# Weight conversion at the start of a fused attention and feed-forward kernel: a third buffer for raw words, exponents through PSUM, rows on two queues, one piece begun ahead

## The chip, the core and the metric

The kernel runs on one core of a Trainium2 chip. The metric is the device time of the whole program in microseconds (us), the median of several runs. The profile is one execution on that core, taken by the hardware profiler. The engines are TensorE (PE in the profile; PEld is its weight load), VectorE (DVE), ScalarE (ACT), GpSimd (POOL) and SyncE (SP, which here only issues transfers).

## The reference

Inputs q, k, v are 8 x 8 x 576 x 64 in float32: batch, heads, sequence, head size. For each batch and head:

```python
scores = scale * np.matmul(q, k.transpose(0, 1, 3, 2))
kth = np.partition(scores, -32, axis=-1)[..., -32:-31]
scores = np.where(scores >= kth, scores, -1000000000.0)
attn = softmax(scores)           # max subtracted, 1e-09 in the divisor
out = np.matmul(attn, v)
```

The heads are put side by side, which gives x of 4608 x 512, and then comes a feed-forward block with weights w_in (512 x 2048) and w_out (2048 x 512):

```python
h = x @ w_in
g = h - np.tanh(h)
y = g @ w_out
```

Each row of scores keeps only what is at least its 32nd largest value. The two weights are handed over as float64. [...] the kernel takes the two 32-bit words of each float64 apart and puts a float32 together.

## The kernel before, in words

**Steps.** The work is cut into 144 steps. A step is a pair of heads and a tile of 128 query rows (or, for the 64 rows that are left over, two pairs of heads). All orders are written out by hand: `run` goes over n from -4 to NS + 3, and in each round emits one stage of several steps: the scores of step n + 1 (`scores`, L224, matmul L233, copy out of PSUM L241), the search of step n (`search`, L244), the mask of step n - 1 (`mask`, L280: tb L290, z L303 on ScalarE and L306 on GpSimd, bad L310), its exponentials (`expo`, L322, L326), the transpose of step n - 2 (on TensorE in `turn_pe`, L389: matmuls L404 and copies L407; or on VectorE in `turn_z`, L365, and `spread_keys`, L377), and the product with v (`values`, L414, matmuls L428, the reciprocals' transpose L436, copy L440, xT L452). [...]

**The search** is VectorE's main work. It takes the minimum and maximum of the two halves of the scores (L263, L264), then four rounds of max (L271) and match-replace (L274), each of which gives the eight next largest. After each of the four rounds it calls `between(i)`, which emits what was planned for that gap: transposes of k and q rows (`turn_rows`, L218), and parts of the weight conversion.

**Feed-forward work** is a list (`work`) of small items (`ffn_h`, matmuls L481, tanh L493, copy L494, subtraction L495; `ffn_o`, matmuls L502, copy L512). `deal` gives them out between the stages, at the rate that `rate` computes from what is due. An item isn't given out before the weight pieces that it uses are converted: `converted[0]` counts these.

**The weight conversion** (`convert`, L136). A piece is 128 rows by 512 columns; there are 32: 0 to 15 are w_in, 16 to 31 w_out. A piece needs a place for raw words (a "slot") with two halves, one for the words as they are and one for the same bytes shifted by three. SyncE issues the two loads (L146, L147). Part 1 of the piece, emitted later: VectorE takes sign and exponent bits out of the high words (L156, into f), ScalarE turns them into a float32 exponent with two instructions (L157 and L158, both from f into f), VectorE takes the mantissa bits from the shifted words (L160), ScalarE scales these (L163). Part 2: VectorE joins sign and exponent (L166, with the raw words and f as inputs, f as output), and GpSimd multiplies both (L169). Part 2 frees the slot, and `load_piece` (L600) at once takes the first free slot that the next piece may use and emits its loads.

**Slots** (L128 to L134). Two slots lie in the tile `spare`, which serves as a transposition buffer later; four lie in the parts of w_out that aren't converted yet. Each has a bound: a slot in w_out[j] may be used only by pieces before that part is itself filled, that is before piece 16, 20, 24 or 28; a slot in `spare` by any piece. `load_piece` takes the first usable slot in the list. So pieces 28 to 31 have only the two slots of `spare`. `zx2` (L115) holds two transposition buffers for later: the first in its own tile, the second in `spare`.

**The plan of the conversion** is `many`: two pieces in step 0, two in step 1, three in each of the steps 2 to 9, four in step 10. Within a step, the parts are spread over the four gaps of the search.

**The start.** Before the first search come, on SyncE's queue: four loads each of the first k rows and q rows (`load_rows`, L196; a row load is 72 KB in runs of 128 bytes), the loads of piece 0, the next k and q rows, piece 1, and so on. The PSUM pool `h_ps` has two buffers with the tag "h", which only the feed-forward products use.

Of the kernel before, what the change touches and what calls it, by code (L numbers as in the profile page):

```python
# [8 lines left out]
AF = mybir.ActivationFunctionType  # L9
ALU = mybir.AluOpType  # L10
FP32 = mybir.dt.float32
I32 = mybir.dt.int32
U32 = mybir.dt.uint32
# [35 lines left out]
def kernel(  # L49
# [9 lines left out]
    nc = tc.nc  # L59
    P = nc.NUM_PARTITIONS  # L60
# [7 lines left out]
    CD = DM // P  # L68
# [6 lines left out]
    WJ = 4  # L75
    FJ = CF // WJ
    scale = 1.0 / float(D) ** 0.5
# [5 lines left out]
    def pool(name, bufs, **kw):  # L83
        return ctx.enter_context(tc.tile_pool(name=name, bufs=bufs, **kw))
# [15 lines left out]
    h_ps = pool("h_ps", 2, space=PS)  # L100
# [9 lines left out]

    NW = 512


    spare = consts.tile([P, 4, NW, 2], U32, name="spare")
    later = spare[:].rearrange("p a n w -> p (a n w)").bitcast(FP32)  # L115
    zx2 = [consts.tile([P, 4 * S], FP32, name="zx")[:], later[:, 0 : 4 * S]]
# [3 lines left out]
    e255 = consts.tile([P, 1], FP32, name="e255")  # L120
    nc.gpsimd.memset(e255[:], 255.0 * 2.0**23)

    def flat(x):
        return x.rearrange("p n w -> p (n w)")

    slots = [(spare[:, i], spare[:, 2 + i], 8 * CD) for i in range(2)]  # L128
    for j in reversed(range(WJ)):
        halves = [  # L130
            flat(w_out[j][:, 2 * i : 2 * i + 2, :]).bitcast(U32).rearrange("p (n w) -> p n w", w=2)
            for i in range(2)
        ]
        slots.append((*halves, (WJ + j) * CD))  # L134

    def convert(piece, slot):  # L136


        j, i = piece // CD, piece % CD
        if j < WJ:  # L140
            src, dst = moe_w_in[i * P : (i + 1) * P, j * NW : (j + 1) * NW], w_in[j][:, i, :]
        else:
            r0 = ((j - WJ) * FJ + i) * P
            src, dst = moe_w_out[r0 : r0 + P, :], w_out[j - WJ][:, i, :]
        raw, shifted, _ = slot
        nc.sync.dma_start(flat(raw), src.bitcast(U32))  # L146
        nc.sync.dma_start(  # L147
            flat(shifted).bitcast(U8)[:, 0 : 8 * NW - 4], src.bitcast(U8)[:, 3 : 8 * NW - 1]
        )
        yield  # L150
        hi = raw[:, :, 1]
        f = thpool.tile([P, NW], FP32, tag="th", name="f")
        fu = f[:].bitcast(U32)


        nc.vector.tensor_scalar(fu, hi, 20, 0x7FF, ALU.logical_shift_right, ALU.bitwise_and)  # L156
        nc.scalar.activation(f[:], fu, AF.Relu, bias=e1151[:], scale=-(2.0**23))  # L157
        nc.scalar.activation(f[:].bitcast(I32), f[:], AF.Relu, bias=e255[:], scale=-1.0)  # L158

        nc.vector.tensor_scalar(  # L160
            dst.bitcast(U32), shifted[:, :, 0], 0x0FFFFFFF, None, ALU.bitwise_and
        )
        nc.scalar.activation(dst, dst.bitcast(U32), AF.Copy, bias=1.0, scale=2.0**-28)  # L163
        yield

        nc.vector.scalar_tensor_tensor(  # L166
            out=fu, in0=hi, scalar=0x80000000, in1=fu, op0=ALU.bitwise_and, op1=ALU.bitwise_or
        )
        nc.gpsimd.tensor_tensor(dst, dst, f[:], ALU.mult)  # L169
        yield  # L170
# [15 lines left out]
    def load_rows(name, b, hp, exact):  # L186

        if b == 0 and hp and not exact:
            x = early[2 * hp - 2 + (name == "q")]
        else:  # L190
            x = ldpool.tile([P, S], FP32, tag=f"{name}in", name=f"{name}in")[:]
        raw[name, b, hp] = x
        src = {"k": k, "q": q}[name]
        for a in range(NG):
            h, d = 2 * hp + a // 2, a % 2 * G
            nc.sync.dma_start(  # L196
                x[a * G : (a + 1) * G, :].rearrange("i (n d) -> i n d", d=G),
                src[b, h, :, d : d + G].rearrange("(n i) d -> i n d", i=G),
            )
# [145 lines left out]
    def spread(n):  # L345

        if steps[n].last:
            rd = rds.pop(n)
            nq = steps[n].nq
            rx = rxs[n] = xpool.tile([P, 2, 2, D], FP32, tag="rx", name="rx")  # L350
            nc.gpsimd.tensor_copy(
                rx[:, 0:nq], rd[:, 0:nq].unsqueeze(3).to_broadcast([P, nq, 2, D])
            )
# [174 lines left out]
    steps, done, work = [], {}, []  # L528
# [38 lines left out]
    def run(exact):  # L567
# [4 lines left out]
        def at(n, fn):  # L572
            todo.setdefault(n, []).append(fn)
# [3 lines left out]
        for i, (b, hp) in enumerate(pairs):  # L577
            n = next(n for n, g in enumerate(steps) if (g.b, g.hp) == (b, hp))
# [18 lines left out]
        pieces = 0 if exact else 2 * WJ * CD  # L597
        free, loaded, converted = list(slots), [], [2 * WJ * CD - pieces]

        def load_piece():  # L600
            k = len(loaded)
            usable = [x for x in free if x[2] > k]
            if k < pieces and usable:
                free.remove(usable[0])
                piece = convert(k, usable[0])
                next(piece)
                loaded.append((piece, usable[0]))

        def part(x, k):
            next(loaded[k][0])  # L610
            if x == 2:
                converted[0] = k + 1
                free.append(loaded[k][1])
                load_piece()

        for _ in slots[NHP:]:
            at(-4, load_piece)
        started = 0
        for m in range(max(many) + 1 if pieces else 0):
            mine = range(started, min(started + many[m], pieces))  # L620
            started = mine.stop
            seq = [(1, k) for k in mine[:1]]
            for k in mine[1:]:
                seq += [(1, k), (2, k - 1)]
            seq += [(2, k) for k in mine[-1:]]
            for i, x in enumerate(seq):
                at_round.setdefault((m, 3 * i // max(len(seq) - 1, 1)), []).append(
                    lambda x=x: part(*x)
                )

        def here(i):
            return 0 <= n + i < NS

        def between(i):
            for fn in at_round.pop((n, i), []):
                fn()
            if i == 0 and here(-2):
                invert(n - 2)
                if not steps[n - 2].pe:
                    turn_z(n - 2)  # L640
# [9 lines left out]
        for u in begun:  # L650
            k = 2 if u.tag == "xT" else 1
# [5 lines left out]
        def rate():  # L657


            have, low, high = len(work), 0.0, None  # L660
            coming = sorted((t, u.n // 8) for u, t in ready.items() if t > n)
            for t, k in coming + [(NS + 4, 0)]:
                r = have / max(t - n, 1)
                high = r if high is None else min(high, r)
                have += k
            for u, t in begun.items():
                if t > n and u in before:
                    need = [i + 1 for i, x in enumerate(work) if x[1] is before[u]]
                    if need:
                        low = max(low, need[-1] / (t - n))  # L670
            return max(low, high)

        credit = 0.0

        def deal(part):
            nonlocal credit
            credit += part * share
            while work and credit > 0 and work[0][0] <= converted[0]:
                work.pop(0)[2]()
                credit -= 1  # L680
            credit = min(credit, 1.0)

        for n in range(-4, NS + 4):
            pe = here(-2) and steps[n - 2].pe
            if here(-3) and not steps[n - 3].pe:
                spread(n - 3)
            for m in (n - 4, n - 3):
                if 0 <= m < NS and steps[m].last and steps[m].lag == n - m:
                    values(m)
            share = rate()  # L690
            if pe:
                w = turn_pe(n - 2)
                next(w)
            if here(-1):
                mask(n - 1, exact)
            if here(0):
                search(n, exact, between)
            elif here(-2):
                between(0)
            if here(-2) and not pe and steps[n - 2].last:  # L700
                spread_keys(n - 2)
            if pe:
                spread(n - 2)
            deal(0.4)
            if here(1):
                scores(n + 1)
            if pe:
                next(w)
            if here(-1):
                expo(n - 1)  # L710
            deal(0.2)
            if pe and steps[n - 2].last:
                values(n - 2)
            deal(0.2)
            for fn in todo.pop(n, []):
                fn()
            deal(0.2)
# [4 lines left out]
    with tc.manual_schedule():  # L722
        run(False)
# [42 lines left out]
```

## Time and profile before

| | value |
|---|---|
| time, median of 3 runs | 1573.74 us (1572.37 to 1576.3) |
| span of the profiled execution | 1571.8 us |
| TensorE busy | 1463.9 us (93%) |
| VectorE busy | 1322.7 us (84%) |
| ScalarE busy | 907.7 us (58%) |
| GpSimd busy | 945.5 us (60%) |
| chain that ended last | TensorE 81%, VectorE 8%, ScalarE 4%, SyncE's queue 3%, GpSimd 2% |
| loads of w_in and w_out pieces, issue to landing | 4.2 to 6.2 us |

How to read it: busy time is an average over stages with different limits. The page cuts the span into 40 equal slices (39.3 us each) and gives the busy tenths of each engine: TensorE is at 2 to 7 tenths in the first five slices and at 8 or 9 from the sixth on. A row of a timeline gives start, duration, engine, line of the program, operation, out<-in and, in brackets, how long the engine had stood idle before it and which instruction or transfer ended that. Releasers are inferred from semaphore events; where an instruction waits for several, the one that came last by the profile is named.

### The profile page before, as it was taken

The numbers are of one execution on the slowest core, as the hardware profiler recorded it, in microseconds if no ns is written. First come the engines' busy times: TensorE is split into PE (matmuls) and PEld (weight loads), VectorE is DVE, ScalarE is ACT, GpSimd is POOL, SyncE is SP. The second block draws the span as 40 slices with busy tenths as digits, with TensorE's granted clock in tenths as the row PEclk, the third lists the DMA queues.
The fourth block names the chain that finished last, engine by engine and source line by source line (L and its number), as shares of the span: only waits on it lengthen the run. The fifth ranks groups of instructions, "written<-read, shape, count | busy, mean of one in ns | idle before, by whom it ended". The sixth has DMA issues, their size and how long they took to land.

```text
span 1571.8 us, 25605 instructions
## 1 busy us (share of the span) xinstructions
PE 1463.9 (93%) x7834; PEld 940.6 (60%) x7834; DVE 1322.7 (84%) x3810; ACT 907.7 (58%) x1637; POOL 945.5 (60%) x1533
## 2 busy tenths in 40 slices
PE   2566699899999999999999999999999999999998
PEld 1355376556566565656666565656666666666675
DVE  7987689999999999998999999998999899874300
ACT  4877577556556565656556565656555565654431
POOL 2777467657567575657467575756566565644521
PEclk9877799999999999999999999999999999999999
DMA  9844112333532334233432343333432334210000
GB/s 248 297 172 168 69 30 56 88 86 65 115 88 61 90 82 91 69 80 75 100 88 62 84 94 83 74 79 76 97 92 61 82 84 96 55 45 7 8 8 16
DMA packets 245009, 134.43 MB, mean 86 GB/s; under 512 B 205440, under 2 KB 205440, under 8 KB 244864
## 3 DMA queue, kind: packets, MB, share of 16 engines
q1 hardware_dynamic: 244864, 132.71, 34.7%
q8 instruction: 64, 1.05, 0.3%
q14 instruction: 81, 0.66, 0.1%
HBM read 61.85 MB, written 9.44 MB: 45 GB/s over the span
## 4 chain that ended last, share of the span: by engine, by line
PE 81%; DVE 8%; ACT 4%; SPq 3%; POOL 2%; DMA 1%; issue 1%; DVEq 0%; ACTq 0%; POOLq 0%
PE hps L481 29%; PE ops L502 29%; PE av L428 9%; PE scps L233 9%; PE zt L404 2%; DVE m L271 2%; DVE ab L274 2%; PE av L436 2%; SPq L196 1%; SPq L385 1%; DVE f L166 1%; ACT z L303 1%; DMA spare<-in_moe_w_out_dram 1%; ACT sc L241 1%; ACT f L157 1%
## 5 line engine op out<-in xcount | busy, mean ns | idle before, releaser
L502 PE MATMUL ops<-w_out,g 128*128 128x512 f32 x1152 | 524.7, 599 | 0.0
L481 PE MATMUL hps<-xT,w_in 128*128 128x256 f32 (+1 forms) x2304 | 476.0, 362 | 0.2 <-POOL xT L452 0.2
L271 DVE MAX8 m<-ab 128x8 f32<-128x288 f32 (+1 forms) x1152 | 464.9, 445 | 0.0
L306 POOL TENSOR_TENSOR z<-sc,z 128x576 f32<-128x576 f32 x288 | 400.0, 1411 | 106.3 <-ACT z L303 106.3
L481 PEld LDWEIGHTS hps<-xT,w_in 128*128 128x128 f32 x2304 | 399.2, 195 | 63.5 <-issue 14.4
L274 DVE MATCH_REPLACE8 ab<-m,ab 128x288 f32<-128x288 f32 x864 | 376.2, 443 | 0.0
L502 PEld LDWEIGHTS ops<-w_out,g 128*128 128x128 f32 x1152 | 210.9, 192 | 232.0 <-issue 229.7
L303 ACT ACTIVATE z<-sc,tb 128x576 f32<-128x576 f32 x288 | 207.8, 770 | 138.3 <-POOL tb L290 138.3
L495 POOL TENSOR_TENSOR g<-g,th 128x512 f32<-128x512 f32 x144 | 183.8, 1276 | 130.2 <-ACT g L494 126.3
L241 ACT COPY sc<-scps 128x1152 f32<-128x1152 f32 x144 | 160.9, 1117 | 121.5 <-PE scps L233 117.0
L326 ACT ACTIVATE z<-z,nb 128x576 f32<-128x576 f32 x288 | 221.7, 775 | 5.3 <-POOL z L306 5.2
L263 DVE TENSOR_TENSOR ab<-scps,sc 128x576 f32<-128x576 f32 x144 | 107.0, 743 | 133.2 <-POOL bad L310 73.3
L233 PE MATMUL scps<-kT,qT 64*128 64x288 f32 (+1 forms) x1280 | 185.5, 439 | 31.0 <-DVE qT L218 28.8
L233 PEld LDWEIGHTS scps<-kT,qT 64*128 64x128 f32 (+1 forms) x1280 | 100.5, 181 | 122.3 <-issue 65.5
L428 PE MATMUL av<-et,vb 128*64 128x256 f32 (+1 forms) x1152 | 133.5, 368 | 39.9 <-ACT et L407 34.2
L493 ACT ACTIVATE th<-hps 128x512 f32<-128x512 f32 x144 | 85.3, 592 | 114.7 <-PE hps L481 107.1
L452 POOL TENSOR_TENSOR xT<-xs 128x256 f32<-128x256 f32 (+1 forms) x72 | 48.0, 667 | 157.2 <-ACT xs L440 157.0
L428 PEld LDWEIGHTS av<-et,vb 128*64 128x64 f32 x1152 | 77.6, 140 | 100.2 <-ACT et L407 37.8
L440 ACT COPY xs<-av 128x512 f32<-128x512 f32 (+1 forms) x88 | 44.7, 508 | 154.9 <-PE av L436 154.8
L336 POOL TENSOR_SCALAR rd<-den 128x2 f32<-128x2 f32 x144 | 33.4, 232 | 146.7 <-ACT z L326 113.1
L266 DVE MAX8 ab<-ab 128x8 f32<-128x288 f32 x288 | 116.4, 445 | 0.0
L264 DVE TENSOR_TENSOR ab<-scps,sc 128x576 f32<-128x576 f32 x144 | 107.4, 746 | 0.0
(59 smaller groups left out, 1319.0 us busy)
## 6 DMA issues: line engine op xcount, KB each, us to landing
et<-spare SPq DMA_DIRECT2D x416, 72.0 KB, 2.0
et<-zx SPq DMA_DIRECT2D x416, 72.0 KB, 2.0
kin<-in_k_dram SPq DMA_DIRECT2D x116, 72.0 KB, 2.4
qin<-in_q_dram SPq DMA_DIRECT2D x116, 72.0 KB, 2.5
vb<-in_v_dram SPq DMA_DIRECT2D x64, 128.0 KB, 2.5
out_dram<-ot SPq DMA_DIRECT2D x32, 256.0 KB, 2.2
spare<-in_moe_w_out_dram SPq DMA_DIRECT2D x11, 512.0 KB, 4.2
spare<-in_moe_w_out_dram SPq DMA_DIRECT2D x11, 511.5 KB, 5.1
```

Of the source, the lines that this page charges most:

```text
L233: nc.tensor.matmul(ps[rows, t, s, 0:S2], qT[g.b, g.hp + i][half(t), qs], kT[g.b, g.hp + i][half(t), ks], start=True, stop=True,)
L241: nc.scalar.copy(sc[:], ps[:, :, :, 0:S2])
L266: nc.vector.max(ab[:, t, S2 : S2 + 8], lo[:, t, :])
L271: nc.vector.max(m[:, t, m8], last[t] if i == rounds - 1 else cur[t])
L274: nc.vector.match_replace(nxt[t], m[:, t, m8], cur[t], NEG)
L303: nc.scalar.activation(zv[:, t, :], scf[:, t, :], AF.Relu, bias=tb[:, t : t + 1], scale=-BIG)
L306: nc.gpsimd.tensor_tensor(zv[:, t, :], scf[:, t, :], zv[:, t, :], ALU.subtract)
L326: nc.scalar.activation(x["zv"][:, t, :], x["zv"][:, t, :], AF.Exp, bias=x["nb"][:, t : t + 1], scale=scale, accum_out=den[:, t : t + 1],)
L428: nc.tensor.matmul(av[half(t), 0, cols], vb[g.b, hp][:, t, c, :] if c < J else vr[g.b, hp][:, t, :], es[:, :, (J + 1) * t + c if c < J els ...
L481: nc.tensor.matmul(cur[u][:, s : s + w], w_in[j][:, c, fo : fo + P], u.xT[:, c, 0:w], start=(c == 0), stop=(c == CD - 1),)
L495: nc.gpsimd.tensor_tensor(g, g, th[:], ALU.subtract)
L502: nc.tensor.matmul(cur[u][:], u.g[o // 1024][:, o % 1024 // 512, o % 512 : o % 512 + P], w_out[f // FJ][:, f % FJ, :], start=(f == 0), sto ...
```

## The change

It has five parts, all in the conversion of weights and in the start. A third slot, `first`, lies in the first transposition buffer (`zx2[0]`), which isn't used before the conversion is over, so seven pieces instead of six can be under way, and three instead of two at the end; `load_piece` takes the usable slot with the earliest bound instead of the first of the list. For the pieces of w_in, L158 writes its exponents into a PSUM tile (`e`, from the pool `h_ps`) instead of into f, and L166 reads them there. Three of the four loads of the first q rows are issued by ScalarE instead of SyncE. Part 1 of piece 0 is emitted in round -1, before the first search, instead of in its first gap. And `deal` compares with the number of pieces converted before the round's search (`usable`) instead of with the number at that moment.

```diff
+    first = zx2[0][:, 0 : 4 * NW].bitcast(U32).rearrange("p (a n w) -> p a n w", a=2, w=2)
     slots = [(spare[:, i], spare[:, 2 + i], 8 * CD) for i in range(2)]
+    slots.append((first[:, 0], first[:, 1], 8 * CD))
...
         nc.scalar.activation(f[:], fu, AF.Relu, bias=e1151[:], scale=-(2.0**23))
-        nc.scalar.activation(f[:].bitcast(I32), f[:], AF.Relu, bias=e255[:], scale=-1.0)
+
+        e = h_ps.tile([P, NW], FP32, tag="h", name="e")[:] if j < WJ else f[:]
+        nc.scalar.activation(e.bitcast(I32), f[:], AF.Relu, bias=e255[:], scale=-1.0)
...
         nc.vector.scalar_tensor_tensor(
-            out=fu, in0=hi, scalar=0x80000000, in1=fu, op0=ALU.bitwise_and, op1=ALU.bitwise_or
+            out=fu, in0=hi, scalar=0x80000000, in1=e.bitcast(U32), op0=ALU.bitwise_and, op1=ALU.bitwise_or
         )
...
-            nc.sync.dma_start(
+            queue = nc.scalar if a and (name, b, hp, exact) == ("q", 0, 0, False) else nc.sync
+            queue.dma_start(
...
             if k < pieces and usable:
-                free.remove(usable[0])
-                piece = convert(k, usable[0])
+                slot = min(usable, key=lambda x: x[2])
+                free.remove(slot)
+                piece = convert(k, slot)
                 next(piece)
-                loaded.append((piece, usable[0]))
+                loaded.append((piece, slot))
...
+        if pieces:
+            at(-1, lambda: part(1, 0))
...
+            seq = [x for x in seq if x != (1, 0)]
...
-            while work and credit > 0 and work[0][0] <= converted[0]:
+            while work and credit > 0 and work[0][0] <= usable:
...
-            share = rate()
+            share, usable = rate(), converted[0]
```

## The prediction

> **What bounds the kernel now.** I read the busy shares in slices first, then busy time by stage, then the waits of VectorE in the first 200 us, then the timeline of single steps. First busy time in four stages; the columns are the stretch, its length, and busy us (instructions) of TensorE, its weight loads, VectorE, ScalarE and GpSimd, then TensorE's granted clock, DMA share and GB/s:
> ```profile
> 0.00:180.00 180.00, 91.08 (x493) 66.08 (x493) 143.30 (x376) 119.02 (x207) 106.44 (x143) 0.81 0.65 207
> 180.00:400.00 220.00, 208.34 (x1191) 135.34 (x1192) 212.74 (x632) 143.74 (x267) 149.01 (x252) 0.99 0.29 63
> 400.00:1400.00 1000.00, 999.68 (x5208) 623.63 (x5207) 927.38 (x2675) 582.81 (x1043) 629.06 (x1048) 1.00 0.37 82
> ```
> From 400 us TensorE has no gap and the change removes no matmul, so nothing is to be won there. From 180 to 400 us VectorE and TensorE are both near full, and that work is not touched either. What can be won is start-up, where TensorE idles 89 of 180 us while the weights are converted: if stage one ends X us sooner, all that follows starts X us sooner. So I count X.
>
> Start-up goes in steps, one search each; a step begins with L263. The same table by step, for steps 0, 1, 4 and 8 to 10 (step 0 begins at 11.76 us):
> ```profile
> 11.76:23.77 12.01, 2.29 (x8) 1.26 (x8) 12.01 (x32) 4.93 (x7) 1.26 (x1) 1.00 1.14 236
> 23.77:36.81 13.04, 3.52 (x14) 2.46 (x15) 12.44 (x33) 7.98 (x14) 7.04 (x9) 1.00 1.08 308
> ...
> 64.33:77.71 13.38, 7.23 (x41) 4.99 (x39) 12.75 (x35) 11.14 (x22) 10.79 (x13) 0.63 0.63 226
> ...
> 120.34:136.65 16.31, 12.13 (x86) 10.76 (x86) 12.84 (x34) 12.01 (x24) 12.15 (x15) 0.81 0.42 144
> 136.65:153.78 17.13, 11.22 (x63) 8.75 (x64) 12.76 (x34) 12.82 (x25) 12.06 (x15) 0.70 0.46 170
> 153.78:180.84 27.06, 12.32 (x38) 5.76 (x35) 14.52 (x38) 12.90 (x24) 10.96 (x14) 0.69 0.33 117
> ```
> VectorE fills steps 0 to 5 (12.75 of 13.38 us), idles 3 to 4 us in steps 7 to 9, and idles 12.5 us of 27.06 in step 10. Its waits up to 200 us say on what (us in total, times, longest):
> ```profile
> DVE f L166 <- ACT f L158: 17.3, 8, 4.4
> DVE f L156 <- DMA spare<-in_moe_w_out_dram: 6.0, 3, 3.3
> DVE kT L218 <- DMA kin<-in_k_dram: 4.9, 1, 4.9
> DVE ab L263 <- ACT sc L241: 3.9, 3, 3.5
> DVE w_out L160 <- DMA spare<-in_moe_w_out_dram: 2.3, 3, 0.8
> ```
> The second and fifth rows are step 10, waiting for raw words; the third and fourth are mostly the start of step 0. The first is 0.63 us a step up to step 6, then 2.8 to 4.4 us in steps 7 to 10. Last, VectorE's own rows around the end of step 3 (start, us):
> ```profile
> 61.79 0.67 DVE L166 SCALAR_TENSOR_TENSOR f<-w_out,f 128x512 uint32<-128x512 uint32 x1
> 62.38 0.82 DVE L271 MAX8 m<-ab 128x8 f32<-128x296 f32 x2
> 63.13 1.28 DVE L166 SCALAR_TENSOR_TENSOR f<-w_out,f 128x512 uint32<-128x512 uint32 x1
> 64.33 0.74 DVE L263 TENSOR_TENSOR ab<-scps,sc 128x576 f32<-128x576 f32 x1
> ```
> The same L166 takes 0.67 or 1.28 us. GpSimd's L169 ran from 62.59 to 63.86, and the slow L166 ends 0.55 us after it: it stood still until GpSimd was done. L263 has one operand in PSUM, runs beside the next L169 (64.54 on), and takes 0.74.
>
> [...] No row here has ScalarE writing PSUM; L158 into SBUF takes 0.72 us. [...] four row issues take 2.01 us on SyncE, and the DMA engines are already 0.78 to 0.91 busy from 2 to 5 us.
>
> **The change, part by part.** "Piece k" is the k-th of 32 weight pieces: 0 and 1 in step 0, 2 and 3 in step 1, then three a step, 28 to 31 in step 10.
>
> *Exponents by way of PSUM (pieces 0 to 15, steps 0 to 5).* L166 then has one SBUF input. Its price from the nearest row: L263, 576 elements in 0.74 us[...]. Nine of the 16 are slow now (1.30, 1.30, 1.30, 1.35, 1.28, 1.35, 1.29, 1.35, 1.27: 11.8 us), so 11.8 - 9 x 0.68 = 5.7 us of VectorE time goes. Is it on the path? In steps 3 to 5 two loops start at the end of a step's last L166: VectorE's own, 6.7 us to the next step's first L166 (64.33 to 71.0), and L169 (GpSimd), rx, the transposes (TensorE), et, z, L157, L158 (ScalarE), 7.2 us (64.41 to 71.64), the 0.63 us wait. Both begin earlier with it, and the two slow L166 lie between the loop's end and its next start, so both savings count whole: 3.8 us over steps 3 to 5. ScalarE then needs 11.1 of about 12.1 us, and the next L263 may wait 0.4 us for the scores' copy, inside the 0.5 us by which VectorE's loop is shorter. Step 2 has one slow L166: 0.6. Steps 0 and 1 are below. Bounds: 5.7 if all counts; about 1 if ScalarE's copy holds the step. L158 into PSUM: I take 0.72[...]. The exponents share two PSUM buffers with the first feed-forward product; a third L158 of a step must await the first L166, which precedes L156 of that piece on VectorE anyway: nothing. The first product comes after piece 15's step.
>
> *First q rows on two queues.* Three of four issues leave SyncE's queue: the last q row is issued 1.6 us sooner (3 x 0.53). But the DMA engines have only 0.22 + 0.20 + 0.09 + 0.11 + 0.05 + 0.08 = 0.75 us idle between 2 and 8 us. Bounds 0.3 and 1.6; I take 0.75. ScalarE's three issues (about 1.5 us) lie before its first copy at 10.61: nothing.
>
> *One piece begun ahead.* L156 and L160 of piece 0 (0.41 each) move into VectorE's 3.54 us gap before the first L263: 0.7 us off step 0. They wait for piece 0's words, behind which the first search stands on VectorE. DMA moves these words between 6 and 10.5 us now; with the 0.75 they land by 10, the scores by 11: no stall, by a small margin.
>
> But steps 0 and 1 can't keep it all: DMA is saturated (share 1.14, 1.08), and piece 3 is already awaited,
> ```profile
> DVE w_in L160 <- DMA w_out<-in_moe_w_in_dram: 0.6, 1, 0.6
> ```
> and its words still come behind the same transfers. So up to there only the 0.75 us is gained, the pair moved and piece 1's L166 going into this wait, and after it piece 3's L166 (0.6): 1.4 together.
>
> *A third place for raw words, tightest deadline first.* Following load_piece by hand: before, pieces 28 to 31 have two places, so 30 is issued after 28 is finished and 31 after 29. After, 30 is issued at the end of step 9, and only 31 in step 10, when 28 is finished. The issues and VectorE's waits now:
> ```profile
> 165.59 0.33 SPq L146 DMA_DIRECT2D spare<-in_moe_w_out_dram  x1
> 170.44 0.43 DVE L156 TENSOR_SCALAR f<-spare 128x512 uint32<-128x512 uint32 x1 [3.30 <-DMA spare<-in_moe_w_out_dram]
> 172.68 0.33 SPq L146 DMA_DIRECT2D spare<-in_moe_w_out_dram  x1
> 176.78 0.43 DVE L156 TENSOR_SCALAR f<-spare 128x512 uint32<-128x512 uint32 x1 [2.55 <-DMA spare<-in_moe_w_out_dram]
> ```
> Step 10 on today's clock: piece 28's L166 still ends at 165.55 (ScalarE's chain sets it, 4.28 us, not touched; the 0.91 us waits before it vanish into that). Then max and replace to 167.1, L156 and L160 of piece 30 to 167.8, L166 of 29 to 168.4, max and replace to 170.0; L156 of 31 waits to 170.44 and L160 to 171.63, as 30's did; L166 of 30 to 172.6, maxes to 173.3, L166 of 31 behind L169 to 174.6. Now 180.84: 6.2 us. Bounds: 3.3 + 0.8 = 4.1 if only the first wait goes, 7.35 if all four. In steps 6 to 9 every piece has 13 us or more to arrive, before and after. The new order sends seven pieces ahead, so the first v rows wait one more megabyte (2.7 us at the 377 GB/s of 36 to 40 us); they are awaited at 44.6 and issued by 34.2: hidden.
>
> *The limit taken before the search* (usable): the order of TensorE's and GpSimd's instructions that the changed kernel writes out is the old one, so nothing.
>
> Sum: 1.4 + 0.6 + 3.8 + 6.2 = 12.0; 1573.7 - 12.0 = 1561.7, said as 1562.
>
> **Rivals.** (a) Only step 10 gains, 6.2 + 0.5: 1567. For it: ScalarE is the next full engine, and DMA is saturated up to 60 us. Against: the loop starts at L166. (b) All gains at their upper bounds, 1.6 + 0.7 + 5.7 + 7.35 = 15.4: 1558.3. Against: piece 3's wait. (c) No change, 1572 to 1574: TensorE's low granted clock (0.63 to 0.9 before 180 us) shifts[...], and it gives back what was won. For: steps 7 to 9 do wait behind 3.6 us bursts of L481. Against: no such work is added. (d) Slower: L166 from PSUM always takes 1.35 (16 x 0.67 - 5.7 = +5), piece 0 stalls the first search by 2, and piece 31 lands so late that step 10 gives 3: 1578. Against: L263's 0.74.
>
> **How the numbers follow.** Forecast 0.55, (a) 0.20, (b) 0.15, (c) 0.07, (d) 0.03. Range 1556.5 to 1568: it holds the forecast and most of (a) and (b); the bounds of 4.1 to 7.35 and 1 to 5.7 reach no further. Faster by over 0.3% (4.7 us): forecast, (b), nearly all of (a), a little of (c): 0.90; within: 0.08; slower: 0.02.
>
> **What would show it.** Right: L166 at 0.68 for pieces 0 to 15 beside GpSimd, still 1.28 for later ones; steps 3 to 5 near 12.1 us; step 10 near 20.8 with one wait for raw words; steps 6 to 9 as before; TensorE gapless from about 390. Wrong: L263 waiting on L241 by more than 0.5 us in each step; L156 of piece 0 or 1 waiting over 1 us; steps 7 to 9 over 17.5 us.

## The result, and the profile after

The changed kernel takes 1561.93 us (median of 4 runs, 1561.04 to 1565.41). Runs of the kernel before, taken with it, have a median of 1573.05 us (1572.32 to 1576.3). The ratio is 0.9929, with a 95% interval of 0.9909 to 0.995: 11.2 us less, where 12 was forecast. The profiled execution has a span of 1560.3 us, against 1571.8.

First busy time by stage in the changed kernel, with stage borders 10 us earlier (columns as in the prediction):

```profile
0.00:170.00 170.00, 89.37 (x498) 65.34 (x499) 140.72 (x379) 121.21 (x212) 105.11 (x145) 0.82 0.67 219
...
390.00:1390.00 1000.00, 999.68 (x5218) 624.96 (x5215) 925.54 (x2669) 584.04 (x1042) 630.20 (x1050) 1.00 0.37 82
```

The first stage is 10 us shorter, and the busy time of the engines differs by 3 us at most. In the middle one, left out here, TensorE and VectorE are busy for 209.55 and 212.12 of 220 us (208.34 and 212.74 before), and the last is what it was. So what went from start-up is mostly idle time, and on VectorE some time in which a slow join (1.27 to 1.35 us instead of 0.67) counted as busy while it stood still. The steps of the changed kernel, 0, 1, 4 and 8 to 10:

```profile
10.82:21.80 10.98, 2.29 (x8) 1.27 (x8) 10.79 (x31) 4.91 (x7) 1.26 (x1) 1.00 1.09 244
21.80:34.77 12.97, 3.07 (x12) 2.01 (x13) 11.91 (x34) 7.90 (x13) 6.88 (x9) 1.00 1.06 302
...
60.96:73.12 12.16, 6.99 (x38) 4.75 (x38) 11.74 (x35) 11.14 (x22) 9.21 (x14) 0.64 0.78 290
...
115.06:131.69 16.63, 12.56 (x86) 11.20 (x86) 12.84 (x34) 12.11 (x24) 12.15 (x15) 0.80 0.35 126
131.69:148.04 16.35, 9.78 (x63) 7.30 (x64) 12.75 (x34) 12.81 (x25) 12.07 (x15) 0.82 0.47 176
148.04:168.40 20.36, 12.98 (x38) 6.27 (x35) 14.13 (x37) 12.82 (x24) 10.98 (x14) 0.75 0.29 104
```

Set against the steps of before (the second column), this gives the account of the profiled execution. The first search starts 0.94 us earlier. The steps then gain:

| | predicted | measured, us |
|---|---|---|
| start of the first search, steps 0 and 1 | 1.4 | 0.94 + 1.03 + 0.07 = 2.04 |
| step 2 | 0.6 | 14.13 - 13.50 = 0.63 |
| steps 3, 4, 5 | 3.8 | 0.70 + 1.22 + 1.12 = 3.04 |
| steps 6 to 9 | 0 | 0.41 - 0.84 - 0.32 + 0.78 = 0.03 |
| step 10 | 6.2 | 27.06 - 20.36 = 6.70 |
| start of step 11 | 12.0 | 180.84 - 168.40 = 12.44 |
| end of the span | 12.0 | 11.5 |

The 0.9 us between the last two rows is mostly lost in step 12 (9.11 us against 8.52). VectorE's waits in the first 190 us of the changed kernel (total us, times, longest):

```profile
DVE f L169 <- ACT f L161: 16.5, 4, 5.7
...
DVE ab L267 <- ACT sc L245: 2.8, 6, 1.2
DVE w_in L163 <- DMA w_out<-in_moe_w_in_dram: 2.1, 3, 1.1
...
DVE w_out L163 <- DMA spare<-in_moe_w_out_dram: 0.5, 1, 0.5
```

Lines are numbered anew: L163 was L160, L169 was L166, L267 was L263, and so on. The 8.3 us of waits for the second matrix's raw words (6.0 and 2.3 before) have shrunk to the 0.5 of the last row. The first row, 17.3 before, is now wholly ScalarE's chain in steps 7 to 10: 16.5 us, where the same four waits were 14.7 (the one of step 10 has grown from 4.28 to 5.69). L267 now waits six times for the copy of the scores, L263 did so three times.

The end of step 3 on VectorE, as it was shown before the change:

```profile
58.51 0.67 DVE L169 SCALAR_TENSOR_TENSOR f<-w_out,e 128x512 uint32<-128x512 uint32 x1
...
59.85 0.66 DVE L169 SCALAR_TENSOR_TENSOR f<-w_out,e 128x512 uint32<-128x512 uint32 x1
60.96 0.76 DVE L267 TENSOR_TENSOR ab<-scps,sc 128x576 f32<-128x576 f32 x1 [0.45 <-ACT sc L245]
```

The second join takes 0.66 us, although GpSimd's L172 ran from 59.31 to 61.91. But 0.45 of the 0.62 us won is then waited away in front of L267. All instructions that write or read the exponents of the first matrix (e) in the changed kernel, by shape, with shortest, median and longest duration in ns:

```profile
L161 ACT ACTIVATE e<-f,e x16: 691/692/692, 11.5 to 83.0; 128x512 int32<-128x512 f32 x16
...
L169 DVE SCALAR_TENSOR_TENSOR f<-w_out,e x10: 657/670/689, 18.3 to 84.3; 128x512 uint32<-128x512 uint32 x10
L169 DVE SCALAR_TENSOR_TENSOR f<-spare,e x4: 667/672/674, 43.5 to 72.1; 128x512 uint32<-128x512 uint32 x4
L169 DVE SCALAR_TENSOR_TENSOR f<-zx,e x2: 665/676/687, 47.7 to 80.0; 128x512 uint32<-128x512 uint32 x2
```

None of the 16 joins is above 0.69 us; nine of them were at 1.27 to 1.35 before. The traces also tell who the neighbour is. In the kernel before, 19 of all 32 joins take 1.27 to 1.36 us, and each of the 19 starts 0.5 to 0.6 us after a GpSimd L169 or L306 that is still running; none of the other 13, at 0.67 to 0.69, does. In the changed kernel, eight of the 16 joins that read PSUM start beside such an instruction, and take 0.66 to 0.69 us all the same. Last, step 10: its issues of raw words, then VectorE's rows that answer to the two waits of 3.30 and 2.55 us.

```profile
148.15 0.33 SPq L147 DMA_DIRECT2D spare<-in_moe_w_out_dram  x1
...
160.14 0.33 SPq L147 DMA_DIRECT2D spare<-in_moe_w_out_dram  x1
```

```profile
158.77 1.35 DVE L169 SCALAR_TENSOR_TENSOR f<-spare,f 128x512 uint32<-128x512 uint32 x1 [5.69 <-ACT f L161]
...
164.56 0.41 DVE L157 TENSOR_SCALAR f<-spare 128x512 uint32<-128x512 uint32 x1
165.50 0.43 DVE L163 TENSOR_SCALAR w_out<-spare 128x512 uint32<-128x512 uint32 x1 [0.54 <-DMA spare<-in_moe_w_out_dram]
```

Piece 30 is issued as step 10 begins, 13 us ahead of its use, and piece 31 when piece 28 is joined. L157 of 31 no longer waits, and L163 waits 0.54 us.

### The profile page after: what moved, and what is told of

Read it like the earlier page. It is cut to its first block, busy times and chain, and to the rows that moved or that the text cites. A ratio compares the mean times of both kernels' runs of the same rounds, so it can differ in the third digit from the quotient of the medians.

```text
span 1560.3 us, 25603 instructions
## 1 busy us (share of the span) xinstructions
PE 1461.8 (94%) x7834; PEld 939.3 (60%) x7834; DVE 1317.6 (84%) x3810; ACT 908.5 (58%) x1637; POOL 942.8 (60%) x1533
## 4 chain that ended last, share of the span: by engine, by line
PE 78%; DVE 9%; ACT 4%; SPq 4%; DMA 2%; POOL 2%; issue 1%; DVEq 0%; ACTq 0%; POOLq 0%
PE hps L485 29%; PE ops L506 28%; PE av L432 9%; PE scps L237 8%; DVE m L275 2%; DVE ab L278 2%; PE zt L408 2%; SPq L389 2%; PE av L440 2%; SPq L200 1%; DVE ab L270 1%; DVE ab L267 1%; DVE ab L268 1%; DMA zx<-in_moe_w_in_dram 1%; ACT z L307 1%
## 5 line engine op out<-in xcount | busy, mean ns | idle before, releaser
L307 ACT ACTIVATE z<-sc,tb 128x576 f32<-128x576 f32 x288 | 207.8, 770 | 138.9 <-POOL tb L294 138.9
L499 POOL TENSOR_TENSOR g<-g,th 128x512 f32<-128x512 f32 x144 | 184.0, 1278 | 129.3 <-ACT g L498 126.6
L245 ACT COPY sc<-scps 128x1152 f32<-128x1152 f32 x144 | 161.1, 1119 | 119.5 <-PE scps L237 114.8
L330 ACT ACTIVATE z<-z,nb 128x576 f32<-128x576 f32 x288 | 221.7, 775 | 5.3 <-POOL z L310 5.2
L267 DVE TENSOR_TENSOR ab<-scps,sc 128x576 f32<-128x576 f32 x144 | 106.9, 743 | 133.0 <-POOL bad L314 74.1
L432 PE MATMUL av<-et,vb 128*64 128x256 f32 (+1 forms) x1152 | 132.2, 365 | 44.0 <-ACT et L411 38.4
L432 PEld LDWEIGHTS av<-et,vb 128*64 128x64 f32 x1152 | 76.5, 138 | 103.7 <-ACT et L411 41.8
```

The lines of the kernel that those rows point to most:

```text
L245: nc.scalar.copy(sc[:], ps[:, :, :, 0:S2])
L307: nc.scalar.activation(zv[:, t, :], scf[:, t, :], AF.Relu, bias=tb[:, t : t + 1], scale=-BIG)
L330: nc.scalar.activation(x["zv"][:, t, :], x["zv"][:, t, :], AF.Exp, bias=x["nb"][:, t : t + 1], scale=scale, accum_out=den[:, t : t + 1],)
L432: nc.tensor.matmul(av[half(t), 0, cols], vb[g.b, hp][:, t, c, :] if c < J else vr[g.b, hp][:, t, :], es[:, :, (J + 1) * t + c if c < J els ...
L499: nc.gpsimd.tensor_tensor(g, g, th[:], ALU.subtract)
```

## The experiments

Each kernel is compared with runs of the kernel before on the same chip; the kernels of one part below were run together. Microseconds given with a ratio are worked out from the ratio, not from the two medians; in the first three kernels below these lie 5.7, 4.0 and 0.3 us apart. Three theories stood at first: the one of the prediction (three gains that add up), that only the third place counts, and that the parts help only together.

**One part at a time.** The third place alone, on the kernel before:

```diff
+    first = zx2[0][:, 0 : 4 * NW].bitcast(U32).rearrange("p (a n w) -> p a n w", a=2, w=2)
+    slots.append((first[:, 0], first[:, 1], 8 * CD))
-                piece = convert(k, usable[0])
+                slot = min(usable, key=lambda x: x[2])
+                piece = convert(k, slot)
```

> Kernel before with the third slot and the tightest-bound choice alone. Theory (gains by part add up, each in its own steps): step 10 falls from 27.1 to about 20.5 us, all other steps stay, L163's wait for piece 31 is under 1 us; time 1566.5 us (-6.5). Rival 1 (only the third slot counts; what steps 0 to 5 gain is given back in steps 7 to 10): 1562 us, as the whole change. Rival 2 (the parts help only together): 1571 us or more.

Measured: 1567.09 us against 1572.79, ratio 0.9958 (0.9944 to 0.9972), 6.6 us. Step 10 takes 19.81 us, steps 3 to 5 stay at 13.36 to 13.39.

The exponents by way of PSUM alone, on the kernel before:

```diff
-        nc.scalar.activation(f[:].bitcast(I32), f[:], AF.Relu, bias=e255[:], scale=-1.0)
+        e = h_ps.tile([P, NW], FP32, tag="h", name="e")[:] if j < WJ else f[:]
+        nc.scalar.activation(e.bitcast(I32), f[:], AF.Relu, bias=e255[:], scale=-1.0)
...
-            out=fu, in0=hi, scalar=0x80000000, in1=fu, op0=ALU.bitwise_and, op1=ALU.bitwise_or
+            out=fu, in0=hi, scalar=0x80000000, in1=e.bitcast(U32), op0=ALU.bitwise_and, op1=ALU.bitwise_or
```

> Kernel before with the exponents of the first matrix through PSUM alone. Theory: the joining instruction takes 0.67 us for all 16 pieces of the first matrix and 0.67 to 1.4 us for those of the second; step 3 to 5 fall from 13.4 to about 12.4 us; piece 1's saving goes into the wait for piece 3's words; time 1568.8 us (-4.3). Rival 1 (given back later): 1573 us, with steps 7 to 10 longer by the same 4 us. Rival 2: 1572 us or more.

Measured: 1568.78 us, ratio 0.9971 (0.996 to 0.9982), 4.6 us. Steps 2 to 5 gain 0.64, 0.69, 1.22 and 1.10 us. Step 10 stays at 26.55, with both its long waits for raw words:

```profile
164.35 0.43 DVE L156 TENSOR_SCALAR f<-spare 128x512 uint32<-128x512 uint32 x1 [2.71 <-DMA spare<-in_moe_w_out_dram]
170.78 0.43 DVE L156 TENSOR_SCALAR f<-spare 128x512 uint32<-128x512 uint32 x1 [2.66 <-DMA spare<-in_moe_w_out_dram]
```

So rival (a), that only step 10 gains, is refuted: this kernel gains nothing to speak of there and is still faster.

The first q rows on two queues and piece 0 begun ahead, both, on the kernel before:

```diff
+            queue = nc.scalar if a and (name, b, hp, exact) == ("q", 0, 0, False) else nc.sync
-            nc.sync.dma_start(
+            queue.dma_start(
...
+        if pieces:
+            at(-1, lambda: part(1, 0))
+            seq = [x for x in seq if x != (1, 0)]
```

> Kernel before with q rows on two queues and piece 0 begun ahead, nothing else. Theory: the first search begins about 0.9 us sooner; at piece 3's shifted words only about 1.4 us are left, since the loads in front of them set that time; time 1571.6 us (-1.4). Rival 1: 1573 us. Rival 2 (each gain counts whole: 0.94 + 0.7): the wait for piece 3 stays at 0.6 us and the time is 1571.3 us or less.

Measured: 1572.5 us, ratio 0.9995 (0.9986 to 1.0003): 0.8 us less, which can't be told from nothing. The three add up to 6.6 + 4.6 + 0.8 = 12.0 us, and the whole change gives 11.2: they help one by one, and the theory that they need each other falls.

The whole change without the third place. It keeps the choice of the tightest bound, which now gives piece 23 a place in the part of w_out that piece 24 fills in the same step: some raw words are written over before they are joined, so some rows of w_out hold other numbers. The instructions and their order are untouched.

```diff
-    slots.append((first[:, 0], first[:, 1], 8 * CD))
```

> Changed kernel without the third slot (the other parts kept, the tightest-bound choice too). Theory: step 10 is back at about 27 us with two waits for raw words; time 1568.4 us (5 us below before, 6.5 above the changed kernel). Rival 1: 1573 us, as before. Rival 2 (parts help only together): 1571 us or more.

Measured: 1568.26 us, ratio 0.9966 (0.9952 to 0.9979), with step 10 at 26.13 us. Taking the third place out of the whole costs about what adding it alone gives. As the choice of the tightest bound was kept here, it is the place that counts and not the choice; the place with the old choice wasn't run. One wait is due to the raw words that are written over, since piece 23's join must now come behind ScalarE's write of piece 24:

```profile
128.71 0.69 DVE L168 SCALAR_TENSOR_TENSOR f<-w_out,f 128x512 uint32<-128x512 uint32 x1 [0.69 <-ACT w_out L165]
```

With it, step 8 takes 16.95 us, against 16.25 to 16.46 in the three kernels above. So this kernel's time is too long by about half a microsecond (an estimate from these steps), which doesn't change the reading.

**Why PSUM helps, and what the start is worth.** A rival for the PSUM part: what helps may be that the join no longer works in place, or that f is free sooner, and not the memory in which the exponents lie. So the exponents go to a buffer of their own in SBUF, on the kernel before:

```diff
-        nc.scalar.activation(f[:].bitcast(I32), f[:], AF.Relu, bias=e255[:], scale=-1.0)
+        e = zx2[0][:, piece % 2 * NW : (piece % 2 + 1) * NW] if j < WJ else f[:]
+        nc.scalar.activation(e.bitcast(I32), f[:], AF.Relu, bias=e255[:], scale=-1.0)
...
-            out=fu, in0=hi, scalar=0x80000000, in1=fu, op0=ALU.bitwise_and, op1=ALU.bitwise_or
+            out=fu, in0=hi, scalar=0x80000000, in1=e.bitcast(U32), op0=ALU.bitwise_and, op1=ALU.bitwise_or
```

> Kernel before with the exponents of the first matrix in a buffer of their own in SBUF (the then unused transposition buffer) instead of in PSUM: the joining instruction no longer reads and writes the same tile, but still has two SBUF inputs. Theory (the slow instances stand still behind a GpSimd instruction that reads SBUF): the joining instruction keeps its two durations, 0.68 and 1.28 to 1.36 us, about nine of 16 slow; steps 3 to 5 stay at 13.4 us; 1573 us. Rival (what was slow is the output lying on the input, or the ScalarE write to SBUF just before it): 0.68 for all 16, steps 3 to 5 at 12.4 us, 1568.5 us as with PSUM.

Measured: 1573.94 us against 1574.0, ratio 1.0001 (0.9993 to 1.001). ScalarE writes these buffers in 0.72 us, as it wrote f. The joins that read them:

```profile
L167 DVE SCALAR_TENSOR_TENSOR f<-w_out,zx x10: 671/680/1337, 36.7 to 92.3; 128x512 uint32<-128x512 uint32 x10
L167 DVE SCALAR_TENSOR_TENSOR f<-spare,zx x6: 685/1299/1343, 21.0 to 87.5; 128x512 uint32<-128x512 uint32 x6
```

The joins are at 0.67 or 1.3 us as before, the same nine of 16 slow, and steps 3 to 5 at 13.36 to 13.39. It is the operand's place in PSUM that counts: with the exponents there, none of the 16 took more than 0.69 us. What it is that a join and its GpSimd neighbour contend for isn't shown by these runs.

The slot and PSUM parts together, without the start and without `usable` (the edits of the first two kernels, together):

> Changed kernel without its start (all first q rows on one queue, piece 0 begun in the first gap) and without the earlier limit on feed-forward items. Theory: the third slot and PSUM add up; the start is worth what it was alone, under 1.5 us; 1561.5 to 1563.5 us. Rival (the start is worth more once PSUM has made VectorE faster, since piece 3's words then bound it): 1564 us or more.

Measured: 1562.31 us, ratio 0.9926 (0.9912 to 0.9939). The two parts carry the whole gain within what can be measured: 11.6 us here and 11.2 with the other edits, each with some 2 us either way, so what those add can't be told from nothing.

More of the first rows on the second queue, on the changed kernel:

```diff
-            queue = nc.scalar if a and (name, b, hp, exact) == ("q", 0, 0, False) else nc.sync
+            queue = nc.scalar if a + hp and (name, b, hp // 2, exact) == ("q", 0, 0, False) else nc.sync
```

> Changed kernel with all q rows of the second pair on ScalarE's queue too. Theory (two queues together move the 128-byte runs faster than one, 183 to 231 GB/s against 126 to 146): the waits for the words of pieces 1 and 3 (0.19, 0.27 and 0.79 us) go, the first search does not begin later; 1561 us. Rival (the DMA engines are full and only their order changes): piece 0's words come later, the first search begins up to 1 us later, 1562.5 us.

Measured: 1561.93 us, ratio 0.9927 (0.9913 to 0.994), no different from the changed kernel's 0.9929. In its trace piece 3's words are awaited by only 0.22 us, but piece 0's land later: its L163 begins at 10.81 instead of 9.17, and the first search straight behind it at 11.15 instead of 10.82. That is what the rival expected, but L163 of piece 0 begins just as late in two kernels that don't have this edit (see below), so the run doesn't decide it.

**What holds the steps now.** Three waits are left: piece 3's words, TensorE's feed-forward work ahead of the transposes in steps 7 to 10, and the slow joins of the second matrix. One edit for each, on the changed kernel, and then all three. Piece 3's loads ahead of the last pair's k rows:

```diff
+                if i == NHP - 1 and not x and not exact:
+                    at(-4, lambda: load_piece())
...
-                if x and i < NHP and not exact:
+                if x and i < NHP - 1 and not exact:
```

> Changed kernel with the loads of piece 3 ahead of the last pair's k and q rows instead of behind them. Theory (piece 3's wait in step 1 is the order of the transfer queue): its two waits (0.27 and 0.79 us) go, step 1 falls to about 11.9 us, nothing else moves; 1561 us, 1 us below the changed kernel. Rival (the DMA engines are full anyway): the wait turns up at the last pair's transposes in step 2, or at pieces 4 to 6; 1562 us.

Measured: 1559.32 us, ratio 0.9918 (0.9902 to 0.9935). Steps 0 and 1 take 11.25 and 11.72 us (10.98 and 12.97 in the changed kernel), but step 2 takes 0.34 more. The interval overlaps that of the changed kernel, so this gain isn't shown.

Up to round 9, feed-forward work is dealt out at two places of a round instead of four, and none is left between the values (L432, L440) and the next round's transposes (L408):

```diff
-            deal(0.4)
+            deal(0.4 if n > 9 else 0.8)
...
-            deal(0.2)
+            if n > 9:
+                deal(0.2)
...
-            deal(0.2)
+            if n > 9:
+                deal(0.2)
```

> Changed kernel with the feed-forward items of rounds up to 9 given out right behind the search's transposes (share 0.8 at once) instead of partly ahead of the next transposes. Theory (in steps 7 to 10 the 3.4 us burst of feed-forward matmuls ahead of the transposes stands in the loop that releases the first joining instruction): steps 7 to 9 fall from 16.6 to 13.0-13.6 us, step 10 by 2 to 3; about 1550 us. Rival 1 (TensorE's own work at its low clock sets these steps): steps 7 to 9 stay above 16, 1562 us. Rival 2 (the scores come too late behind the moved items): VectorE waits for the scores' copy instead, 1558 us or more.

Measured: 1553.07 us, ratio 0.9879 (0.9862 to 0.9895). In step 10 of the changed kernel, TensorE runs, straight after the matmul L440,

```profile
150.08 3.62 PE L506 MATMUL ops<-w_out,g 128*128 128x512 f32 x4
153.50 1.91 PE L408 MATMUL zt<-ident,z 128*128 128x128 f32 x8
```

and in step 10 of this kernel:

```profile
143.87 1.92 PE L408 MATMUL zt<-ident,z 128*128 128x128 f32 x8
145.58 2.71 PE L506 MATMUL ops<-w_out,g 128*128 128x512 f32 x4
```

The transposes (L408) no longer stand behind a 3.62 us burst. Behind them, in the changed kernel, come the copies of et (ScalarE idle 3.95 us, then from 154.65), z (155.93), L158 (157.27), L161 (158.01), and at 158.77 the L169 that had waited 5.69 us. Here that L169 waits 2.27 us, and step 10 takes 16.63 instead of 20.36 us; steps 7 to 9 take 14.44, 14.35 and 14.89. That is more than I had expected of them: GpSimd's small tb stands behind its own feed-forward subtraction (L499, 1.28 us), and ScalarE's L307 now waits for it, 0.85 us in step 8 and 1.65 in step 9.

The exponents of the second matrix by way of PSUM too, in the pool of the transposes:

```diff
-        e = h_ps.tile([P, NW], FP32, tag="h", name="e")[:] if j < WJ else f[:]
+        e_ps, tag = (h_ps, "h") if j < WJ else (zt_ps, "zt")
+        e = e_ps.tile([P, NW], FP32, tag=tag, name="e")[:]
```

> Changed kernel with the second matrix's exponents through PSUM too, in the transposes' two buffers. Theory (the joining instructions of steps 6 to 10 lie in the loop as those of steps 3 to 5 do): 1.2 us less in each of steps 6 to 9 and in step 10; 1556 us. Rival 1 (in those steps the loop is set by TensorE and ScalarE): 1561 us. Rival 2: the ninth transpose and the product with v now stand behind the joining instruction that reads their buffer, steps 7 to 10 are longer by 1 to 2 us each; 1567 us.

Measured: 1557.1 us, ratio 0.9906 (0.9889 to 0.9922). All 32 joins take 0.66 to 0.69 us. Step 10 takes 17.84 us. Steps 6 to 10 are shorter than in the changed kernel by 0.82, 0.77, 2.00, 0.99 and 2.52 us, where 1.2 each was expected, and step 11 is 1.91 longer. The interval overlaps that of the changed kernel a little, so this gain isn't certain by the timed runs alone.

The three together:

> The three edits together on the changed kernel. Theory: steps 6 to 9 are then set by ScalarE (12.2 us busy a step) at 12.4 to 12.8 us; 1546 us. Rival: two of the three undo each other (moved items in front of the ninth transpose, which also waits for the exponents' buffer), 1552 us or more.

Measured: 1548.86 us (1548.07 to 1550.16), ratio 0.9854 (0.9837 to 0.987). It is the fastest version: 23 us less than the kernel before, twice what the change gives. It is 3 us short of what was expected. The profile shows where: steps 6 to 9 take 13.15, 12.27, 13.38 and 13.73 us against 12.4 to 12.8 expected, step 10 takes 16.2, hardly less than the 16.63 of the dealing alone, and step 11 8.86 instead of the changed kernel's 7.71. Why they do wasn't tried.

## Why the prediction was right

The two parts that carry the gain, the third place and the joins, worked as the prediction had them, and each was worth by itself what its steps were to give. That the sum came so near is in part luck: in this pair of executions the start and step 10 gave 1.1 us more than their terms and steps 3 to 5 gave 0.8 less, and in steps 6 to 9 moves of up to 0.8 us cancel.

**Step 10 (predicted 6.2, measured 6.70; alone 6.6).** Right by its steps. Piece 30 is issued at the end of step 9, 31 after 28, and one wait for raw words is left. That wait had been put at what piece 30's words cost before, for both instructions (L156 to 170.44, L160 to 171.63 on the old clock). It is 0.54 us for one of them: the first load is there 4.4 us after its issue at most (160.14 to 164.56), the second after 5.0 (160.52 to 165.50). Counted from the end of piece 28's join, this L163 begins after 5.38 us, where the prediction had 6.08: 0.7 us too dear. The longer wait in front of that join takes 0.3 of it back (it ends 12.08 us after the step's start, 11.77 before).

**The joins (0.68 predicted, 0.67 measured).** The 0.68 was my estimate, right to 0.01 us: the fast L166 of the kernel before took 0.67 to 0.69, and L263, the nearest row with an operand in PSUM, 0.74 for 576 elements instead of 512. L161 into PSUM takes 0.692 us, where L158 into SBUF took 0.722.

**Steps 3 to 5 (predicted 3.8, measured 3.04).** The mechanism held; this term is too large by 0.8. The prediction said that "both savings count whole" and that the wait for the scores' copy stays "inside the 0.5 us by which VectorE's loop is shorter". Measured, L267 waits 0.45, 0.35 and 0.43 us at the ends of these steps. The second join's saving of 0.6 us so reaches the step's end by only 0.2. The rest shows one step later, where the first L169 comes 6.76 us after the step's start (step 4) instead of 7.31. So step 3, which has no such step ahead of it, gains only 0.70, and 0.41 of what step 5 earned lands in step 6, where I had put nothing. Together it is 3.45 of 3.8. In step 4 ScalarE has the step: it is busy 11.14 of 12.16 us and goes without a gap from L307 at 64.90 to the second L330 at 73.84. Its copy L245 in that row, from 71.92, is what VectorE waits for.

**Steps 0 and 1 (predicted 1.4, measured 2.04 in one execution).** The first search comes 0.94 us earlier, where the prediction counted 0.75 us of idle DMA engines. The nearness is luck: single executions differ by as much. With the old start the first search begins at 11.16 to 11.80 us (five kernels, mean 11.53), with the changed kernel's start at 10.59 to 11.54 (seven, mean 10.95). And the step behind the 0.75 was wrong: their share isn't capped at 1 (the table in the prediction already had 1.14), so "1 minus share" isn't idle time, and 1.14 and 1.08 don't show that DMA is "saturated" (the changed kernel has 1.52 from 4 to 5 us). What it did hold is shown below. The two moved instructions wait for their words as predicted, and in the changed kernel's trace the search isn't held up: L163 of piece 0 begins at 9.17 us, not after 10. But the "small margin" of the prediction isn't always there. In the kernel without the third place, whose start is the same, these words land later; the copy of the scores is done at 10.27 us, and the first search begins only behind the moved instruction:

```profile
10.79 0.43 DVE L162 TENSOR_SCALAR w_in<-w_out 128x512 uint32<-128x512 uint32 x1 [1.94 <-DMA w_out<-in_moe_w_in_dram]
11.13 0.75 DVE L266 TENSOR_TENSOR ab<-scps,sc 128x576 f32<-128x576 f32 x1
```

It begins 0.86 us after the end of the copy there. In the kernel with all three edits it is the same, with 0.16 us. The gain of the start goes in part also into the wait for piece 3, 0.79 us long, and the landing of that transfer varies. L160 of piece 3 (L163 in the changed kernel) begins at 32.32 us in the kernel before, at 34.78 in the kernel with exponents in SBUF, whose loads are the same ones, and at 30.92 in the changed kernel. A difference of 1 us in steps 0 and 1 can't be read from single executions, and the timed runs of this part alone give 0.8 us, with an interval from 2.2 less to 0.5 more.

**Steps 6 to 9 (predicted 0, measured 0.03).** Right in sum, and by luck. Step 6 gains the 0.41 from step 5, step 7 loses 0.84, step 8 loses 0.32 and step 9 gains 0.78. Step 7 moves with the granted clock of TensorE. These are its first 16 feed-forward matmuls, which stand ahead of the transposes, in the kernel before, in the changed kernel, and in the kernel before with the third place alone:

```profile
106.53 3.14 PE L481 MATMUL hps<-xT,w_in 128*128 128x128 f32 x16
100.41 3.62 PE L485 MATMUL hps<-xT,w_in 128*128 128x128 f32 x16
105.35 1.95 PE L483 MATMUL hps<-xT,w_in 128*128 128x128 f32 x16
```

The mean granted clock of step 7 was 0.86, 0.70 and 0.97 in these, and the step took 15.85, 16.68 and 14.56 us. It is at 14.56 or 14.57 with 1.95 us for these matmuls in five of the kernels above, four of them the kernel before with a part of the change or with exponents in SBUF; at 15.85 to 15.94 with 3.14 to 3.22 us in three; at 16.68 and 17.07 with 3.62 us in two. In step 9, the first 16 take 2.85 us in the changed kernel and 3.62 before. So what rival (c) feared does happen in single steps; it gave back 0.84 us in one and won 0.78 in another. Why the clock is low in a step of one execution and high in that of another stays open.

**The end.** Start-up's 12.44 us aren't kept whole, as "all that follows starts X us sooner" had it: step 12 gives back 0.6, where L267 waits 1.50 us for GpSimd's bad, against 0.94 before. But step 12 takes 8.4 to 9.1 us in the kernels above, 9.11 with the start alone, so this belongs to the execution more than to the change; its cause wasn't tried.

**`usable`.** The order of instructions is the old one, and the kernel without it and without the start has the same time. It wasn't run alone, so that it is worth nothing isn't shown by itself.

## What to carry to other kernels

Where one instruction takes 0.67 us in some places of a program and 1.3 in others, look at what runs beside it: here the instances at 1.3 stood still for a neighbour. Moving one operand to PSUM made it 0.67 every time, and the same move into SBUF changed nothing. Work out, by hand, when a buffer comes free for each of the last pieces of a stream: the place that was missing cost 6.6 us at the one point where only two were left. And after a gain look at who waits next: here it was work with no hurry (a feed-forward burst) in front of transposes on which the chain hung, and putting it elsewhere was worth some 8 us more.

## What the runs showed that I had not expected

The first row loads are bound by issuing. In the kernel before, one queue issues a 72 KB row load every 0.53 us, which is some 139 GB/s, and the transfers move at just this pace. Here are two windows of 1 us (the last column is GB/s, the one before it the DMA share), in the kernel before:

```profile
3.00:4.00 1.00, 0.00 (x0) 0.00 (x0) 0.00 (x0) 0.00 (x0) 0.00 (x0) 1.00 0.80 128
4.00:5.00 1.00, 0.00 (x0) 0.00 (x0) 0.08 (x1) 0.00 (x0) 0.00 (x0) 1.00 0.91 146
```

and in the changed kernel, where ScalarE issues three of the loads:

```profile
3.00:4.00 1.00, 0.00 (x0) 0.00 (x0) 0.00 (x0) 0.61 (x1) 0.00 (x0) 1.00 1.33 206
4.00:5.00 1.00, 0.00 (x0) 0.00 (x0) 0.00 (x0) 0.00 (x0) 0.00 (x0) 1.00 1.52 231
```

The same loads move at 206 and 231 GB/s. Over all the kernels above, these two windows have 127 to 146 GB/s in the five with one queue and 205 to 252 in the eight with two. So a share of 0.8 to 0.9 didn't mean that the DMA engines had only a tenth or two left.

The second issuer saved issue time. SyncE alone issued the first eight row loads until 4.90 us; in the changed kernel its five are out at 3.28 and ScalarE's three at 2.29. What I had not seen is that issue time was the limit there. It is worth little in this kernel all the same: the start alone gave 0.8 us, which can't be told from nothing.
